# A recurrent attention with a mixing layer on one core: r and k of the first batch by token-parity halves, the logarithm of w and the last tile by halves, and a new order of the work

## The chip, the core and the metric

The kernel runs on one core of a Trainium2 chip. The core has five instruction queues that work side by side: TensorE (PE: matrix multiplies, and the loads of their weights), VectorE (DVE), ScalarE (ACT), GpSimd (POOL) and SyncE (SP, which here issues nearly all transfers). On-chip data lies in SBUF; PE writes its results into PSUM, from where DVE or ACT copies them ("evicts" them). The time is that of one execution on the device, in microseconds; a kernel is judged by the median of several runs.

## The reference

```python
state = zeros((B, H, D, D))                       # B 4, H 8, S 768, D 48
for t in range(S):                                # k, v, r: [B, H, S, D]; w, u: [H, D]
    cur = einsum('bhd,bhe->bhde', u[None] * k[:, :, t], v[:, :, t])
    y[:, :, t] = einsum('bhd,bhde->bhe', r[:, :, t], state + cur)
    state = w[None, :, :, None] * state + einsum('bhd,bhe->bhde', k[:, :, t], v[:, :, t])
x = y.transpose(0, 2, 1, 3).reshape(B, S, H * D)  # [4, 768, 384]
theta = x @ w_theta                               # [384, 384]
zr, zi = x * cos(theta), x * sin(theta)
yr = einsum('ts,bsd->btd', w_tok_r, zr)           # w_tok_r, w_tok_i: [768, 768]
yi = einsum('ts,bsd->btd', w_tok_i, zi)
u = x + yr + yi
out = u + maximum(u @ w_ch, 0)                    # [4, 768, 384], float32
```

## The kernel before

**Tiling.** The 768 tokens of a batch are three pairs of chunks of 128 tokens; with four batches there are twelve pairs, numbered g = 0 to 11. Within a pair the recurrence is turned into multiplies: r is scaled by powers of w (`wpow`) and k by inverse powers (`wpinv`, or `wpinvj` in the first batch), so that the decayed scores are a masked product of the two, and a 48x48 state per head is carried from chunk to chunk.

**One pair (`attention`).** r, k and v are loaded (`load_runs`, `load_kv`), r and k are scaled into `Rw` and `Kw` (L567, L580 and L583), PE transposes them in blocks of 128 by a multiply with the identity (`flips`, L530), and the results are evicted into `RT` and `KT` (L289 on ACT, L291 on DVE). Then come the scores (L631), their masks into `mAT` (L637), the elementwise product `PD` (L644, L650) and its head sums `dg` for the term with u (L659), `yd` (L666), the state updates (L690, evicted into `Sb`), the outputs (L730, L735) added into `x` (L742), the transposed `xT`, the product with w_theta (L760), its sine and cosine (L764, L767), and `zr`, `zi` (L770, L773). `xT` is made by PE for g under 6 and by a DMA transpose on SP after that (`turn`, L543).

**First batch.** In the first batch (`pj`) partition p of a loaded tile holds the tokens 2p and 2p+1 of a pair, side by side, for r, k and v. Index n is the parity of the token. The scales write both parities in one instruction of 128x768 elements; eight flips fill one PSUM tile of 128x1024 bf16, and one eviction writes them with the parities woven together. v is spread back to chunks by multiplies with a 0/1 matrix (`spread_v`, L615).

**Mixing (`mixing`).** The token weights are transposed by PE (L514). For each chunk, twelve multiplies (six parts of two, L791) sum both mixings in one PSUM tile; DVE adds x into `un` (L800); `un` is transposed into `uT`, by PE for g under 4 and for the last pair, by DMA otherwise; three multiplies with w_ch give f (L817); DVE takes the maximum with zero and adds `un` into `fin` (L821); SP stores it (L825). The last pair is flipped and stored one chunk at a time.

**Start.** w is loaded as one row and spread over the partitions by a float32 multiply with ones (L419), whose logarithm is taken in place in PSUM by ACT (L422). Six exponentials with a scale per partition (L428) make `wpow`, `wpinvj` and `wpinv`. `wS` (L454, POOL) scales the state.

**The order.** Each step is a task with its reads and writes. The table `ORDER` gives all tasks in the sequence in which they are issued, with the engine of each (0 PE, 1 DVE, 2 ACT, 3 POOL, 4 SP) and the PSUM tile of each result (eight tiles of 2 KB per partition). An engine runs its tasks in that sequence, each with its waits for its inputs and for the tile's previous reader. The costs and priorities in the task list have no effect on a table that is written out. Among PE's tasks stand 108 pairs of filler multiplies of zeros (`warm_up`, L834), most in the first 31 us and the rest near the end.

Of the kernel before, what the change touches and what calls it, by code (L numbers as in the profile page):

```python
# [15 lines left out]
F32 = mybir.dt.float32  # L16
BF16 = mybir.dt.bfloat16
Alu = mybir.AluOpType
# [9 lines left out]
    (0, 2), (4, 1), (13, 3), (2, 1), (3, 1), (16, 0, 7), (1, 2), (146, 4), (14, 3), (17, 0, 5),  # L28
    (7, 2), (145, 4), (8, 3), (10, 3), (9, 1), (32, 0, 2), (5, 1), (33, 0), (18, 2), (34, 0),
    (144, 4), (20, 2), (35, 0), (153, 3), (36, 0), (37, 0), (23, 2), (38, 0), (39, 0), (15, 3),  # L30
    (24, 2), (40, 0), (41, 0), (22, 2), (154, 0, 6, 0), (12, 3), (186, 4), (150, 1), (19, 2), (42,
    0), (21, 2), (11, 1), (43, 0), (6, 1), (44, 0), (25, 0, 3), (187, 4), (45, 0), (46, 0), (151,
    0, 5), (26, 1), (30, 1), (27, 2), (147, 1), (47, 0), (167, 0, 4), (152, 2), (48, 0), (49, 0),
    (50, 0), (168, 1), (51, 0), (188, 4), (52, 0), (53, 0), (28, 2), (54, 0), (155, 2), (55, 0),
    (189, 1), (31, 3), (56, 0), (148, 0, 3), (156, 2), (169, 0), (149, 2), (190, 0, 0), (229, 4),
    (192, 1), (57, 0), (58, 0), (59, 0), (191, 2), (60, 0), (61, 0), (157, 0, 1, 7), (170, 1),
    (62, 0), (63, 0), (163, 1), (64, 0), (228, 4), (193, 0, 6), (158, 1), (65, 0), (66, 0), (67,
    0), (195, 2), (68, 0), (69, 0), (164, 0, 5), (159, 1), (70, 0), (71, 0), (160, 0, 3, 4), (165,
    2), (194, 2), (230, 4), (166, 3), (196, 0, 1, 0), (161, 1), (72, 0), (73, 0), (209, 0, 7),
    (198, 2), (162, 1), (197, 2), (171, 0, 6), (140, 4), (234, 1), (74, 0), (210, 2), (75, 0),  # L40
    (76, 0), (202, 0, 3, 1), (29, 2), (199, 0, 0, 4), (172, 1), (231, 3), (173, 0, 5), (280, 4),
    (201, 1), (77, 0), (211, 0), (203, 1), (235, 0, 6), (272, 4), (237, 2), (78, 0), (79, 0),
    (174, 1), (80, 0), (81, 0), (82, 0), (83, 0), (212, 1), (84, 0), (236, 2), (232, 0, 4), (142,
    4), (205, 1), (85, 0), (86, 0), (87, 0), (251, 0, 7), (268, 4), (233, 2), (204, 1), (281, 3),
    (175, 0, 6), (200, 1), (88, 0), (141, 2), (206, 0, 1), (276, 4), (89, 0), (90, 0), (247, 1),
    (91, 0), (238, 0, 3, 0), (207, 2), (252, 2), (176, 1), (208, 3), (241, 0, 5, 4), (292, 4),
    (248, 0, 1), (240, 2), (243, 1), (213, 0, 7), (143, 2), (92, 0), (215, 0, 6), (242, 1), (249,
    2), (273, 2), (244, 0, 0, 4), (269, 3), (214, 1), (93, 0), (288, 4), (181, 0, 5), (239, 2),
    (216, 1), (270, 0, 1), (277, 2), (250, 3), (246, 1), (94, 0), (294, 4), (177, 0, 3), (271, 1),
    (182, 2), (217, 0, 4), (183, 2), (245, 1), (253, 0, 7), (293, 4), (218, 2), (297, 3), (95, 0),  # L50
    (96, 0), (97, 0), (254, 1), (278, 0, 6), (255, 0, 0), (178, 2), (184, 1), (282, 0, 4), (179,
    2), (284, 4), (256, 1), (223, 0, 5), (289, 2), (283, 1), (185, 3), (257, 0, 0), (296, 4),
    (180, 1), (219, 0, 7), (224, 2), (258, 2), (279, 1), (298, 0, 4), (98, 0), (274, 0, 3), (220,
    2), (333, 4), (300, 3), (99, 0), (221, 2), (100, 0), (290, 0, 0), (275, 1), (225, 2), (448, 0,
    6), (291, 1), (295, 4), (263, 0, 1), (299, 2), (222, 1), (449, 0), (285, 3), (441, 0, 0),
    (226, 1), (264, 2), (361, 4), (301, 0, 3), (265, 2), (227, 3), (259, 0, 4), (302, 1), (101,
    0), (442, 0), (260, 2), (266, 1), (443, 0), (363, 4), (261, 2), (450, 0), (310, 1), (267, 3),
    (286, 0, 1), (303, 2), (262, 1), (451, 0), (349, 4), (102, 0), (444, 0), (287, 1), (304, 0, 7,
    3), (307, 0, 4, 5), (314, 0, 1), (337, 4), (366, 3), (308, 1), (445, 0), (315, 2), (452, 0),
    (305, 1), (453, 0), (362, 4), (446, 0), (454, 1), (462, 0, 7), (311, 0, 4), (334, 3), (306,  # L60
    1), (463, 0), (357, 4), (312, 2), (350, 2), (464, 0), (447, 1), (313, 3), (465, 0), (466, 0),
    (402, 4), (316, 0), (335, 0, 4), (317, 1), (467, 0), (336, 2), (338, 3), (351, 0, 6), (468,
    1), (455, 0, 0), (352, 2), (318, 0, 3), (309, 1), (359, 4), (369, 3), (339, 0, 1), (367, 0,
    4), (319, 1), (345, 4), (340, 2), (320, 0, 7), (456, 1), (469, 0, 6), (368, 2), (321, 1),
    (470, 0), (341, 4), (370, 0, 0), (407, 3), (358, 2), (471, 0), (371, 1), (322, 0, 1), (364,
    4), (360, 2), (472, 0), (379, 1), (473, 0), (323, 2), (376, 0, 3, 7), (365, 4), (373, 0, 4,
    5), (346, 2), (377, 1), (474, 0), (324, 0, 0), (378, 1), (342, 2), (403, 4), (457, 0, 1),
    (475, 1), (328, 0, 7), (374, 1), (476, 0, 3), (404, 4), (329, 2), (380, 0, 6), (459, 0, 4),
    (477, 1), (381, 2), (325, 2), (375, 1), (343, 0, 6), (326, 2), (372, 3), (353, 4), (480, 0,
    3), (458, 1), (330, 2), (478, 0, 5), (327, 1), (382, 3), (344, 2), (347, 0, 1), (504, 4),  # L70
    (460, 1), (383, 0, 0), (348, 2), (479, 1), (408, 0, 6), (387, 0, 4), (481, 1), (384, 2), (410,
    3), (483, 0, 1), (331, 1), (405, 4), (484, 0), (409, 2), (388, 1), (389, 0, 5), (385, 0),
    (485, 0), (390, 1), (354, 2), (406, 4), (486, 0), (332, 3), (386, 1), (487, 0), (411, 0, 5),
    (505, 4), (355, 0, 3), (412, 1), (391, 0, 7), (509, 3), (356, 2), (488, 0), (420, 1), (506,
    4), (490, 0, 4), (392, 2), (414, 0, 6, 0), (417, 0, 5, 3), (415, 1), (491, 0), (544, 4), (413,
    3), (492, 0), (489, 1), (493, 0), (419, 1), (421, 0, 7), (494, 0), (495, 0), (422, 1), (416,
    1), (461, 4), (423, 3), (424, 0, 6), (510, 0, 1), (418, 1), (425, 2), (426, 0, 0), (507, 4),
    (496, 1), (511, 2), (629, 0, 3), (512, 3), (427, 1), (428, 0, 7), (622, 0, 5), (546, 4), (429,
    1), (103, 0), (397, 0, 0), (430, 0, 7), (398, 2), (497, 0, 1), (549, 3), (545, 4), (399, 2),
    (393, 0, 6), (431, 2), (513, 0, 4), (400, 1), (508, 4), (623, 0), (394, 2), (514, 1), (436, 0,  # L80
    7), (395, 2), (401, 3), (630, 0), (498, 1), (437, 2), (432, 0, 0), (547, 4), (396, 1), (438,
    2), (550, 0, 1), (522, 1), (433, 2), (499, 0, 6), (434, 2), (548, 4), (439, 1), (440, 3),
# [145 lines left out]
def pe_op(ns):  # L228
    return (ns, 217)
# [27 lines left out]
def build(ctx, tc, nc, r, k, v, w, u, moe_w_theta, moe_w_tok_r, moe_w_tok_i, moe_w_ch, out):  # L257
# [90 lines left out]
    def setup():  # L348
# [40 lines left out]
        def pads(ts):  # L389
            for t in ts:  # L390
                nc.gpsimd.memset(t[:, :, :, D:], 0.0)
# [494 lines left out]
```

## Time and profile before

| what | value |
|---|---|
| median of 5 runs | 140.5 us (139.0 to 140.79) |
| profiled execution | 138.66 us, of which span 137.0 us |
| granted TensorE clock, by the profile | 1.0 |
| PE, DVE, ACT, POOL busy in the span | 133.1, 106.9, 77.3, 86.3 us |
| the fillers, L834 | 216 multiplies |
| DMA | 27.6 MB, 202 GB/s mean |

The profile is of one execution. The page gives each engine's busy time, groups of instructions by line with their count, total and mean duration, and the idle time before them with what ended it. A multiply's duration contains its pipeline, so multiplies overlap and the distance between two starts is shorter than the duration of one: 163 ns for 384 columns and 56 ns for 128 columns at full rate. The chain goes back from the last instruction to what released it, and names what stood on the path at each time.

### The profile page before, as it was taken

The page shows a single profiled execution, that of the slowest core. Times are in us where ns is not written, and L with a number is a line of the kernel's source. Part 1 is how long each engine was busy: PE and PEld are TensorE (multiplying, and loading weights), DVE is VectorE, ACT ScalarE, POOL GpSimd, SP SyncE. Part 2 cuts the span into 40 slices and gives each one's busy share as a digit, 9 for nine tenths or more (in the row PEclk, how much of TensorE's full clock was granted, in tenths as well). Part 3 has the DMA queues.
Part 4 walks back from the last instruction along what each step waited for, and adds up shares of the span by engine and source line. Part 5 has one row for each costly group of instructions (what it writes and reads, how often), then busy time and mean ns, then how long its engine had stood idle before and what let it go on. Part 6 is the DMA issues. An engine that isn't in the chain of part 4 may idle for free.

```text
span 137.0 us, 4123 instructions
## 1 busy us (share of the span) xinstructions
PE 133.1 (97%) x1670; PEld 96.3 (70%) x1670; DVE 106.9 (78%) x208; ACT 77.3 (56%) x142; POOL 86.3 (63%) x77
## 2 busy tenths in 40 slices
PE   6999999999999999999999999999999997999995
PEld 4688798886678677686676866667677674666684
DVE  1399899988878898859986989797997897254750
ACT  3869799998559797379552429843018332310010
POOL 7703674999999199599999738689492084040000
PEclk9999999999999999999999999999999999999999
DMA  4999999999899999999999849598973947304761
GB/s 97 272 262 263 305 337 346 166 287 222 253 295 321 161 272 187 269 207 167 187 274 162 192 77 224 119 209 225 224 198 63 263 146 114 115 0 89 228 219 43
DMA packets 72445, 27.60 MB, mean 202 GB/s; under 512 B 67049, under 2 KB 70890, under 8 KB 72426
## 3 DMA queue, kind: packets, MB, share of 16 engines
q1 hardware_dynamic: 72400, 27.34, 87.3%
q8 instruction: 13, 0.21, 0.7%
q14 instruction: 6, 0.05, 0.1%
q10 hardware_dynamic: 26, 0.00, 0.0%
HBM read 20.06 MB, written 4.72 MB: 181 GB/s over the span
## 4 chain that ended last, share of the span: by engine, by line
PE 88%; DMA 8%; DVE 2%; ACT 0%; issue 0%; ACTq 0%; DVEq 0%
PE bank L791 30%; PE bank L530 11%; PE bank L834 10%; PE bank L760 8%; PE bank L817 8%; PE bank L631 4%; PE bank L690 4%; DMA uT<-un 3%; PE bank L735 3%; DMA xT<-x 3%; PE bank L514 3%; PE bank L730 2%; PE bank L659 2%; DVE mAT L637 1%; PE bank L419 1%; PE bank L615 1%
## 5 line engine op out<-in xcount | busy, mean ns | idle before, releaser
L791 PE MATMUL bank<-zi,WiT 128*128 128x384 bf16 x144 | 33.7, 326 | 0.0
L637 DVE TENSOR_TENSOR mAT<-bank,mask 128x512 bf16<-128x512 f32 x48 | 30.9, 681 | 3.5 <-PE bank L631 3.2
L791 PE MATMUL bank<-zr,WrT 128*128 128x384 bf16 x144 | 33.2, 326 | 0.0
L666 POOL TENSOR_TENSOR yd<-dg,vb 128x768 bf16<-128x768 f32 x12 | 18.1, 1506 | 18.0 <-ACT vb L289 6.2
L773 POOL TENSOR_TENSOR zi<-x,sin 128x768 bf16<-128x768 bf16 x12 | 19.7, 1641 | 6.2 <-ACT sin L764 5.9
L764 ACT ACTIVATE sin<-bank 128x384 bf16<-128x384 f32 x24 | 11.8, 496 | 14.9 <-PE bank L760 12.1
L567 POOL TENSOR_TENSOR Rw<-ld,wpow 128x768 bf16<-128x768 f32 x10 | 18.8, 1881 | 0.2 <-DVE mAT L637 0.2
L834 PE MATMUL bank<-zeros 128*128 128x128 bf16 x216 | 18.1, 231 | 0.0
L791 PEld LDWEIGHTS <-WiT 128*128 128x128 bf16 x144 | 12.8, 97 | 6.9
L791 PEld LDWEIGHTS <-WrT 128*128 128x128 bf16 x144 | 12.7, 97 | 6.9
L583 POOL TENSOR_TENSOR Kw<-ld,wpinv 128x768 bf16<-128x768 f32 x9 | 16.4, 1817 | 0.9 <-DMA ld<-in_k_dram 0.9
L770 DVE TENSOR_TENSOR zr<-bank,x 128x384 bf16<-128x384 f32 x24 | 13.0, 550 | 5.0 <-ACT bank L767 5.0
L821 DVE SCALAR_TENSOR_TENSOR fin<-bank,un 128x384 f32<-128x384 f32 x24 | 12.9, 551 | 4.4 <-PE bank L817 4.3
L834 PEld LDWEIGHTS <-zeros 128*128 128x128 bf16 x216 | 14.2, 103 | 3.0 <-issue 2.0
L817 PE MATMUL bank<-Wch,uT 128*128 128x384 bf16 x72 | 14.8, 326 | 0.8 <-DMA uT<-un 0.8
L760 PE MATMUL bank<-Wth,xT 128*128 128x384 bf16 x72 | 15.3, 326 | 0.1
L289 ACT ACTIVATE RT<-bank 128x1024 bf16<-128x1024 bf16 x12 | 12.3, 1031 | 5.3 <-PE bank L530 5.1
L800 DVE TENSOR_TENSOR un<-bank,x 128x384 bf16<-128x384 f32 x24 | 13.1, 551 | 2.2 <-PE bank L791 1.7
L742 DVE TENSOR_TENSOR x<-bank,yd 128x384 bf16<-128x384 f32 x24 | 12.8, 551 | 0.8 <-PE bank L735 0.6
L767 ACT ACTIVATE bank<-bank,pi 128x384 f32<-128x384 f32 x24 | 13.2, 565 | 0.0
L289 ACT ACTIVATE Sb<-bank 64x192 bf16<-64x192 f32 x20 | 6.5, 324 | 8.2 <-PE bank L690 8.0
L817 PEld LDWEIGHTS <-uT 128*128 128x128 bf16 x72 | 6.6, 98 | 4.8 <-DMA uT<-un 1.2
(96 smaller groups left out, 215.3 us busy)
## 6 DMA issues: line engine op xcount, KB each, us to landing
ld<-in_r_dram SPq DMA_DIRECT2D x12, 384.0 KB, 5.3
out_dram<-fin SPq DMA_DIRECT2D x11, 384.0 KB, 2.8
ld<-in_k_dram SPq DMA_DIRECT2D x18, 192.0 KB, 4.7
ld<-in_v_dram SPq DMA_DIRECT2D x18, 192.0 KB, 4.8
ld<-in_moe_w_tok_i_dram SPq DMA_DIRECT2D x6, 384.0 KB, 5.8
ld<-in_moe_w_tok_r_dram SPq DMA_DIRECT2D x6, 384.0 KB, 6.7
ld<-in_v_dram SPq DMA_DIRECT2D x3, 384.0 KB, 5.5
ld<-in_k_dram SPq DMA_DIRECT2D x3, 384.0 KB, 6.2
```

The costliest lines, as they stand in the source:

```text
L289: nc.scalar.activation(dst, src, Act.Copy)
L530: nc.tensor.matmul(bank16(tok)[:, i * C:(i + 1) * C], s, ident, is_transpose=True, start=(i == 0), stop=(i == n - 1))
L567: P.add(mul(g, 2.15), lambda e: eng_of[e].tensor_mul(Rw[:, :, :, :D].transpose([0, 2, 1, 3]), Ls[ir].rearrange("p (h n d) -> p h n d", h=H ...
L583: eng_of[e].tensor_mul(Kw[:, :, :, :D].rearrange("p a h d -> p (a h) d"), Ls[ik].rearrange("p (a d) -> p a d", d=D), wpinv.rearrange("p a ...
L637: P.add({DVE: dve_op(4 * C)}, lambda e, tk=tk[hi], c=c, hi=hi: nc.vector.tensor_mul(mAT[:, c, hi], bank(tk).rearrange("p (h t) -> p h t", ...
L666: P.add({POOL: pool_op(2 * HD, 1.7)}, lambda e: eng_of[e].tensor_mul(yd.rearrange("p a (h d) -> p (a h) d", h=H), wide(dg, D), vb.rearrang ...
L760: nc.tensor.matmul(bank(th)[:, :HD], xT[:, ND * c + dk, :], Wth[:, dk, :], start=(dk == 0), stop=(dk == ND - 1))
L767: P.add({ACT: act_op(HD, True, True)}, lambda e, th=th: nc.scalar.activation(bank(th)[:, :HD], bank(th)[:, :HD], Act.Sin, bias=pi2), use=[th],
L773: P.add({POOL: pool_op(2 * HD, 1.9)}, lambda e: eng_of[e].tensor_mul(zi[:, 2 * pr:2 * pr + 2], x[:, 2 * pr:2 * pr + 2], sn), rd=xk + [("si ...
L791: nc.tensor.matmul(bank(tm)[:, :HD], WT[:, so, to * C:(to + 1) * C], z[:, so], start=(so == 0 and part == 0), stop=(part == 2 * NP - 1 and ...
L817: nc.tensor.matmul(bank(tf)[:, :HD], uT[:, ND * t + dk, :], Wch[:, dk, :], start=(dk == 0), stop=(dk == ND - 1))
L834: nc.tensor.matmul(bank("warm")[:, :C], zeros, zeros, start=True, stop=True, skip_group_check=True)
```

## The change

**r and k of the first batch.** Each scale becomes two instructions, one per parity, of 384 elements each, which may run on DVE or POOL. Each half is flipped by four multiplies into a PSUM tile of its own, and evicted by itself, on ACT or DVE, into every second element of `RT` or `KT`. The keys of `Rw`, `Kw`, `RT` and `KT` are per parity. All later users wait for both halves. Pairs of the other batches are scaled and flipped as before.

**Logarithm of w.** The float32 multiply and the logarithm are done in two halves of 192 columns with a PSUM tile each; the logarithm goes into a new SBUF tile `lnw`, from which all six exponentials read.

**Last tile.** Chunk 1 of the last pair computes f in two column halves in two PSUM tiles, each with its own add and its own store.

**Order.** The whole table is new. The first loads are k, r, v of the first pair instead of v, k, r. Seven of the twelve scale halves stand on DVE and five on POOL (one of the second pair's k, all four of the third pair). 19 filler pairs stand before the first flip, 79 in all before the last multiply of f (before: 15 and 76), and 3 of them between the two halves of the last f. On SP the last stores are: second half of the last chunk, the chunk before it, first half of the last chunk. The planner's cost of a DMA transpose is changed from 1500 to 2000, which acts on nothing but the table.

```diff
+        for n in range(2):
+            q = slice(n * HD // 2, (n + 1) * HD // 2)
+            P.add({PE: pe_op(430)}, lambda e, n=n, q=q: nc.tensor.matmul(
+                bank(("w", n))[:, :HD // 2], ones, w_row[:, q], start=True, stop=True),
+                rd=["ones", "w_row"], wr=["wlog"], acq=[(("w", n), 1)], prio=-200)
+            P.add({ACT: act_op(HD // 2)}, lambda e, n=n, q=q: nc.scalar.activation(
+                lnw[:, q], bank(("w", n))[:, :HD // 2], Act.Ln),
+                rd=["table"], use=[("w", n)], wr=[("lw", n)], prio=-190)
...
-            P.add({ACT: act_op(HD, True, True)}, lambda e, i=i, dst=dst: nc.scalar.activation(
-                dst, bank("w")[:, :HD].rearrange("p (h d) -> p h d", h=H), Act.Exp,
+            P.add({ACT: act_op(HD, False, True)}, lambda e, i=i, dst=dst: nc.scalar.activation(
+                dst, lnw.rearrange("p (h d) -> p h d", h=H), Act.Exp,
                 scale=tok_f[:, i:i + 1]),
...
-        P.add({SP: (1600, 1500)}, lambda e: nc.sync.dma_start_transpose(out=dst, in_=src),
+        P.add({SP: (1600, 2000)}, lambda e: nc.sync.dma_start_transpose(out=dst, in_=src),
...
+    def mul1(g, rate):
+        return {POOL: pool_op(HD, rate), DVE: dve_op(HD)}
...
+        def halves(nm, w_key, wt, src4, ld, Xw, kx, XT, kxt, pri):
+            for n in range(2):
+                P.add(mul1(g, 2.15), lambda e, n=n: eng_of[e].tensor_mul(
+                    Xw[:, n, :, :D], src4[:, :, n, :], wt[:, :, n, :]),
+                    rd=L2(ld) + [(w_key, n)], wr=[kx[n]], prio=pri, lock=SHARED,
+                    name=nm[0].lower() + "scale")
+            for n in range(2):
+                flips(XT[:, :, :, n], [Xw[:, n, 2 * hp:2 * hp + 2, :] for hp in range(HP)],
+                      ("T" + nm[0], g, n), pri, [kx[n]], [kxt[n]], nm,
+                      {ACT: act_op(4 * C), DVE: dve_op(4 * C)})
...
         if pj:
             flat_kt = KT.rearrange("p a h t -> p (a h t)").rearrange("p (h m) -> p h m", h=HP)
-            flips(flat_kt.rearrange("p h (m n) -> p h m n", n=2),
-                  [Kw[:, n, 2 * hp:2 * hp + 2, :] for hp in range(HP) for n in range(2)],
-                  ("TK", g), pb, [kK], [kT], "KT", {ACT: act_op(8 * C)},
-                  lambda t: t.rearrange("q (h n) p -> q h p n", n=2))
+            halves("RT", "wpow", wpow, r4, ir, Rw, kRs, RTn, rt_keys, pb - 1)
+            halves("KT", "wpinvj", wpinvj, k4, ik, Kw, kKs,
+                   flat_kt.rearrange("p h (m n) -> p h m n", n=2), kTs, pb)
...
+                cut = 2 if g == B * NP - 1 and t == 1 else 1
+                for j in range(cut):
+                    tf = ("f", g, t, j)
+                    q = slice(j * HD // cut, (j + 1) * HD // cut)
+
+                    def chan(e, t=t, tf=tf, q=q):
+                        for dk in range(ND):
+                            nc.tensor.matmul(bank(tf)[:, :q.stop - q.start],
+                                             uT[:, ND * t + dk, :], Wch[:, dk, q],
+                                             start=(dk == 0), stop=(dk == ND - 1))
...
+                    if cut == 2:
+                        P.add({SP: (300, 2000)}, lambda e, t=t, q=q: nc.sync.dma_start(
+                            out=out[b, (2 * pr + t) * C:(2 * pr + t + 1) * C, q],
+                            in_=fin[:, t, q]), rd=[("fin", g % 2, t, j)],
+                            wr=[("out", g, t, j)], prio=-2e6, name="out")
```

## The prediction

> **What bounds the kernel now.** I read the page first (busy time, slices, groups), then the chain that ended last, then the timeline of the first 31 us and of the last 10.
>
> ```profile
> PE 133.1 (97%) x1670; PEld 96.3 (70%) x1670; DVE 106.9 (78%) x208; ACT 77.3 (56%) x142; POOL 86.3 (63%) x77
> PE 88%; DMA 8%; DVE 2%; ACT 0%; issue 0%; ACTq 0%; DVEq 0%
> L834 PE MATMUL bank<-zeros 128*128 128x128 bf16 x216 | 18.1, 231 | 0.0
> ```
>
> Busy share and chain both say PE. L834 is the filler: 108 pairs of multiplies of zeros, at fixed places in the order, so PE runs them whether or not it would have been idle. The chain, in order of time:
>
> ```profile
> 2.40 1.61 PE bank L419 x2
> 4.01 2.25 PE bank L834 x20
> ...
> 8.40 0.45 PE bank L530 x8
> ...
> 79.11 4.45 DMA xT<-x
> 83.61 0.66 PE bank L760 x3
> ...
> 111.68 4.51 DMA uT<-un
> 116.23 0.66 PE bank L817 x3
> ...
> 119.98 6.83 PE bank L791 x42
> ...
> 131.70 3.57 PE bank L834 x64
> ```
>
> To be seen: 64 fillers in 3.57 us are 56 ns each, the first 20 took 112 ns, and up to 8.2 us they stay slow, so PE starts at half rate. From there PE runs without a hole (42 mixing multiplies in 6.83 us, 163 ns each) but for two transposes by DMA. The end of the kernel is therefore a count of what stands in PE's order, plus its waits, plus what follows the last f.
>
> **The change, part by part.** The profiled execution took 138.66 us: its span of 137.0 and 1.66 around it. It lies 1.3% under the median of the runs (140.5), so I sum against 138.66 and carry the difference to 140.5.
>
> 1. *Logarithm by halves, r and k by halves.* The multiply L419 is two passes in 1.61 us; half of it ends near 3.2, so its logarithm (0.47 us whole, about 0.31 a half) is done while PE multiplies the other half, and the exponentials start near 4.4 instead of 4.56. Key loads now come first and should land at 4.4, when v landed before. The first scaled half of k can then be ready near 5.6 and both halves of r near 7.7 (384-element DVE operations take 0.55, half of a 0.95 scale 0.47 to 0.55); before they ended at 7.07 and 9.52. Does PE get there earlier? Before the first flip, PE's order now holds 19 filler pairs instead of 15 with the spreading of v and the small transpose between them. From 4.05, 38 multiplies at 0.107 (20 in 2.31, less the last one's length) end at 8.1: where the first flip stands today (8.24). The earlier data is thus worth nothing by itself; the fillers hide it, and they would hide a lateness of 0.9 us.
>
> 2. *PE's count to the last f.* At 8.2 us the kernel before has behind it 15 filler pairs, the spreading of v (0.33 at full rate) and the small transpose (0.20). The kernel after has 19 pairs and owes those 0.53. Ahead of its last f lie 79 pairs in all, not 76: 60 left against 61, less 0.11. Sum +0.42. Adding up the rows task by task to the first mixing multiply gives +0.15 instead, since some small gaps of today fall away. I take +0.3 (range 0 to 0.5). Halving flips adds no multiplies: eight of 56 ns become two times four; their evictions (1.02 us for 1024) become two of about 0.52 on ACT, or on DVE between 0.36 (half of the contiguous copy's 0.69) and 0.67 (the 512-element mask operation); I take the mask's, as the writes are strided.
>
> 3. *Scales on POOL.* Five of the twelve halves of r and k go to POOL: one of the second pair's k, then four of the third pair's in a row. A whole scale on POOL took 1.82, so a half is about 0.95. Two rows show more:
>
> ```profile
> 10.09 1.46 POOL L454 TENSOR_TENSOR wS<-wR,bmask 128x384 f32<-128x384 f32 x1 [3.77 <-ACT wR L441]
> 10.78 1.58 DVE L580 TENSOR_TENSOR Kw<-ld,wpinvj 128x768 bf16<-128x768 f32 x1
> 16.46 2.46 POOL L567 TENSOR_TENSOR Rw<-ld,wpow 128x768 bf16<-128x768 f32 x1 [0.22 <-DVE mAT L637]
> ```
>
> A 384-element multiply on POOL took 1.46 beside a DVE scale that itself took 1.58 instead of 0.95. The Trainium skill (SBUF — State Buffer, "Who interferes with whom") says that DVE with two SBUF inputs and POOL reading SBUF hold one port pair as a lock, the later waiting for the whole instruction, and that DVE with one SBUF input doesn't contend. The 2.46 fits: 1.82, plus the rest of a DVE scale that ran from 16.29 to 17.24. By the rule, the half of k at 10.6 (its load lands at 10.54, fifth as now) waits for DVE's scale of r, and PD (two SBUF inputs) then waits for it: PD ends near 12.5 instead of 11.6, the first mask near 13.1, and the flip that takes that mask's bank, at 12.7 in PE's order, waits 0.5. The four later halves lie beside masks, x and S, which read PSUM, and stay at 0.95. By the row of 1.46 alone the four would end at 15.6 + 5.84 = 21.4 and their flips wait 1.4 more. I take the rule, less what gaps give back: +0.3, bounds 0 and 2.0.
>
> 4. *New order in the middle.* The two DMA waits cost PE 0.81 (row of L817) and between 0.1 and 0.2 (at 83.6), up to 1.2 by the spacing of the multiplies; I take 1.0. PE work between the producing multiply and the first user, by durations of the rows: the xT of the eighth pair 5.3 us before, 6.9 after, so its wait goes. The uT of the ninth pair 4.6 before, with nearly 1.0 of wait, so 5.6 are needed; now 5.3: 0.3 stay. The last three (4.1, 4.2, 4.9 before, without a wait) are 4.4, 4.55, 4.55. A transpose took 2.7 to 4.5 us to land, so one of them can wait 0.5 where it doesn't today. SP's queue runs in order, and each transpose sits behind loads and stores that are ready before it in both orders. Everything else in the middle (evictions on DVE and ACT, bank reuse) is hidden by PE's work now and moves everywhere; I cost it at nothing, with 0.8 if a few come late. Sum -0.8, range -1.2 to +0.5.
>
> 5. *Tail.* Between the two half products of the last tile stand three filler pairs (in the count above), and DVE takes the second half's add first, then the whole tile, then the first half. From the last multiply, DVE ends after about 0.76 (the whole add of 0.55 is still running) against 0.66 today: +0.1. A half-size store follows:
>
> ```profile
> 131.25 1.11 DVE L821 SCALAR_TENSOR_TENSOR fin<-bank,un 128x384 f32<-128x384 f32 x2 [0.43 <-PE bank L817]
> 131.54 3.74 PE L834 MATMUL bank<-zeros 128*128 128x128 bf16 x64
> ```
>
> The last add ends at 132.36, the span at 137.0: 4.6 us are the store and the close. The skill (DMA: Bandwidth & Descriptors, "Anatomy of one DMA") fits a fixed 2.0 us plus bytes over 436 GB/s, for another queue's path; 98 KB less would save 0.22. The rows speak against it: 384 KB stores landed in a median 2.8 us, the two of 192 KB in 3.6. One more store in the row costs SP 0.34. I take -0.2, so -0.1 for the tail (range -0.4 to +0.4).
>
> Sum: +0.3 +0.3 -0.8 -0.1 = -0.3. 138.66 becomes 138.36; 140.5 becomes 140.2.
>
> **The rivals.**
> - *A, likeliest (0.51): gains and costs cancel.* 140.2, by itself 139.2 to 141.4. For it: PE's count is fixed, and fillers stand where the change would show.
> - *B, faster (0.27): the stalls go and nothing comes for them.* Port collisions fall beside fillers (0), waits -1.1, store by half its bytes -0.3, count +0.1: -1.3, so 139.2, down to 138.6. For it: all transposes but the last three have 5.3 us of work or more to cover them. Against: those three stay under 4.6.
> - *C, slower (0.22): the shared port in the first 22 us.* Four POOL halves in a row feed the third pair's flips; PE reaches the last r flip at 20.05. They start at 15.6, so it decides at a mean of 1.09 us each. At 1.46 they cost 1.4; the yd ahead of them may be late too (one took 1.84 instead of 1.48), say 0.2; with the earlier 0.5 that is 2.1 instead of 0.3: +1.5, so 142.0. Against: DVE does masks then.
> - *The halves do nothing at all* is inside A: step 1 already gives them no time.
>
> **How the numbers follow.** About 1% is what a measurement of this kernel can tell from no change (the five runs spread over 1.3%). B reaches under 139.1 about four times in five, C over 141.9 rather more than half the time, A seldom on either side. Faster 0.24, same 0.60, slower 0.16. The range takes A and most of B and C: 138.7 to 142.0.
>
> **What would show it.** Step 1: the first flip on PE stands within 0.3 of 8.2, with DVE's scales done before it. Step 2: the first mixing multiply at 30 to 31. Step 3: POOL halves near 0.95, one near 1.4, PD of the first pair ending after 12.2. Step 4: no wait of PE on xT of the eighth pair, under 0.5 on uT of the ninth. Step 5: the span ends 4.2 to 4.8 after the last add. The prediction is wrong if scores or flips of the second and third pair wait more than 1 us, if PE waits in the middle for evictions, or if the half-rate time of PE shifts by more than 1 us.

## The result, and the profile after

| | before | after |
|---|---|---|
| median of the runs beside each other | 139.62 us (79 runs, 137.85 to 141.08) | 138.87 us (44 runs, 137.86 to 139.62) |
| profiled execution, span | 138.66, 137.0 us | 139.27, 137.6 us |

After over before is 0.998, with a 95% interval from 0.9964 to 0.9995. A later set of runs gave 0.9933 (0.9911 to 0.9956), with medians of 139.02 and 139.79. All ratios leave out runs more than 1.5% above the fastest of their kernel: 30 of the 79 in the first set, by their times, and none in the later one. Over all runs of the first set the ratio of the means is 0.9945, and that of the medians 0.9946. So the change is a gain of between 0.05 and 0.9%, under the 1% bound of the forecast. It is real, and the forecast of no change missed it. The forecast difference was -0.3 us; the ratio of 0.998 makes it just that, and the medians differ by 0.75. The absolute 140.2 was too high from the start: the five runs that I had for the kernel before lay 0.9 above the median of 79. The fastest runs of the two kernels are equal (137.85 and 137.86) and the slowest are 1.46 apart, so in the main the change takes away long executions of the kernel before.

The two profiled executions point the other way: the one of the kernel before is among its faster ones, the one of the changed kernel is above its median. Much of what follows is about why they differ among themselves.

The page of the changed kernel: busy time, the chain's shares by engine, and the filler's group.

```profile
PE 134.0 (97%) x1675; PEld 98.7 (72%) x1675; DVE 109.6 (80%) x222; ACT 76.9 (56%) x140; POOL 85.5 (62%) x77
PE 81%; DMA 7%; DVE 6%; issue 2%; POOL 1%; ACT 1%; SPq 0%; DVEq 0%
L862 PE MATMUL bank<-zeros 128*128 128x128 bf16 x216 | 18.9, 238 | 0.0
```

PE is as busy as before, but DVE and POOL have 7% of the chain, not 2%. Its timeline from 5 to 14 us (start, duration, engine, line, operation; in brackets the idle time before it):

```profile
7.00 0.55 DVE L583 TENSOR_TENSOR Rw<-ld,wpow 128x384 bf16<-128x384 f32 x1
7.78 0.63 PE L535 MATMUL bank<-ident,Rw 128*128 128x128 bf16 x4
...
9.82 0.84 PE L862 MATMUL bank<-zeros 128*128 128x128 bf16 x12
...
10.58 1.00 POOL L583 TENSOR_TENSOR Kw<-ld,wpinvj 128x384 bf16<-128x384 f32 x1 [2.22 <-DMA ld<-in_k_dram]
10.62 1.84 DVE L583 TENSOR_TENSOR Rw<-ld,wpow 128x384 bf16<-128x384 f32 x2
12.39 0.68 DVE L659 TENSOR_TENSOR PD<-RT,KT 128x1024 bf16<-128x1024 bf16 x1
```

The first flip stands at 7.78, with both halves of r ready 0.23 before. PE runs at half rate until about 9.8 here (until 8.2 in the kernel before). Two DVE halves that should take 1.0 take 1.84 beside one POOL half, so PD ends at 13.07. The chain between 100 and 120 us:

```profile
102.57 5.23 DMA out_dram<-fin
...
112.38 4.67 DMA uT<-un
...
117.10 1.15 PE bank L835 x6
```

A store that took 5.23 us to land held DVE's next add for 1.52 us, and with it the masks and scores behind (PE stood 0.5 us near 108). The transpose for the ninth pair's f still took 4.67, but PE waited only 0.3 for it instead of 0.97. Last, the tail:

```profile
131.68 1.09 DVE L841 SCALAR_TENSOR_TENSOR fin<-bank,un 128x192 f32<-128x192 f32 x3 [0.61 <-PE bank L835]
...
132.06 3.40 PE L862 MATMUL bank<-zeros 128*128 128x128 bf16 x58
132.07 0.34 SPq L847 DMA_DIRECT2D out_dram<-fin  x1
132.53 1.55 SPq L853 DMA_DIRECT2D out_dram<-fin  x1
134.18 0.38 SPq L847 DMA_DIRECT2D out_dram<-fin  x1
```

SP needed 1.55 us, not 0.37, to issue the second of the three last stores, so the half store went out 1.4 us after its add (132.77), and the span ended 4.8 after that add.

### The profile page after: what moved, and what is told of

The parts are those of the page before. It is cut to its first block, busy times and chain, and to the rows that moved or that the text cites. A ratio compares the mean times of both kernels' runs of the same rounds, so it can differ in the third digit from the quotient of the medians.

```text
span 137.6 us, 4149 instructions
## 1 busy us (share of the span) xinstructions
PE 134.0 (97%) x1675; PEld 98.7 (72%) x1675; DVE 109.6 (80%) x222; ACT 76.9 (56%) x140; POOL 85.5 (62%) x77
## 4 chain that ended last, share of the span: by engine, by line
PE 81%; DMA 7%; DVE 6%; issue 2%; POOL 1%; ACT 1%; SPq 0%; DVEq 0%
PE bank L806 28%; PE bank L535 10%; PE bank L862 10%; PE bank L835 7%; PE bank L775 7%; PE bank L646 4%; DMA out_dram<-fin 4%; DMA uT<-un 3%; PE bank L750 3%; PE bank L519 3%; PE bank L705 3%; PE bank L745 2%; DVE mAT L652 1%; PE bank L674 1%; PE bank L424 1%
## 5 line engine op out<-in xcount | busy, mean ns | idle before, releaser
L862 PE MATMUL bank<-zeros 128*128 128x128 bf16 x216 | 18.9, 238 | 0.0
L841 DVE SCALAR_TENSOR_TENSOR fin<-bank,un 128x384 f32<-128x384 f32 (+1 forms) x25 | 13.0, 535 | 6.8 <-PE bank L835 5.2
L599 POOL TENSOR_TENSOR Rw<-ld,wpow 128x768 bf16<-128x768 f32 x9 | 16.3, 1817 | 3.3 <-DMA ld<-in_r_dram 3.3
L291 ACT ACTIVATE RT<-bank 128x1024 bf16<-128x1024 bf16 (+1 forms) x14 | 12.7, 924 | 6.3 <-PE bank L535 6.1
L862 PEld LDWEIGHTS <-zeros 128*128 128x128 bf16 x216 | 14.9, 108 | 1.6 <-issue 0.7
L835 PE MATMUL bank<-Wch,uT 128*128 128x384 bf16 (+1 forms) x75 | 15.3, 320 | 0.1
L782 ACT ACTIVATE bank<-bank,pi 128x384 f32<-128x384 f32 x24 | 13.2, 559 | 0.0
L775 PEld LDWEIGHTS <-xT 128*128 128x128 bf16 x72 | 6.5, 97 | 3.6
```

The source lines that it names most:

```text
L599: P.add(mul(g, 2.15), lambda e: eng_of[e].tensor_mul(Rw[:, :, :, :D].transpose([0, 2, 1, 3]), r4, wpow), rd=L2(ir) + [("wpow", 0), ("wpow" ...
L775: nc.tensor.matmul(bank(th)[:, :HD], xT[:, ND * c + dk, :], Wth[:, dk, :], start=(dk == 0), stop=(dk == ND - 1))
L782: P.add({ACT: act_op(HD, True, True)}, lambda e, th=th: nc.scalar.activation(bank(th)[:, :HD], bank(th)[:, :HD], Act.Sin, bias=pi2), use=[th],
L835: nc.tensor.matmul(bank(tf)[:, :q.stop - q.start], uT[:, ND * t + dk, :], Wch[:, dk, q], start=(dk == 0), stop=(dk == ND - 1))
L841: nc.vector.scalar_tensor_tensor(fin[:, t, q], bank(tf)[:, :q.stop - q.start], 0.0, un[:, t, q], op0=Alu.max, op1=Alu.add),
L862: nc.tensor.matmul(bank("warm")[:, :C], zeros, zeros, start=True, stop=True, skip_group_check=True)
```

## The experiments

Ratios are to the kernel before, with 95% intervals. In the trace, a queue of its own carries packets of 16 KB, one for about every 256 instructions of PE (198 to 311 by count in the kernel before) and 13 in all for PE's 1675 multiplies and as many weight loads: PE's program. The Trainium skill (Runtime: NRT & Kernel Launch, "Instruction fetch mechanics") states such a refill in 16 KiB blocks of 256 instructions, by DMA; the count here agrees. "Theory F" is that these fetches hold up transfers.

**The tail, and the kernel without any filler.** The second and third kernel were meant to lose only the fillers behind the last f:

```diff
-                for _ in range(2):
+                for _ in range(0 if i >= 76 else 2):     # kernel before; 79 in the changed kernel
```

The function runs after its loop has ended, when `i` is 107, so both kernels lost all 108 pairs. The expectations speak of the smaller edit. The first kernel has no edit; the fourth stores the last tile whole:

```diff
-                        P.add({SP: (300, 2000)}, lambda e, t=t, q=q: nc.sync.dma_start(
-                            out=out[b, (2 * pr + t) * C:(2 * pr + t + 1) * C, q],
-                            in_=fin[:, t, q]), ...
+                        P.add({SP: (300, 2000)}, lambda e, t=t, j=j: j or nc.sync.dma_start(
+                            out=out[b, (2 * pr + t) * C:(2 * pr + t + 1) * C, :],
+                            in_=fin[:, t]), ...
```

> The changed kernel unaltered, as the yardstick for its variants on the same chip. Every theory: 0.998 of the kernel before, 0.995 to 1.001. What differs between executions is shown by its profile: theory F (fetch in the tail, see the next kernel) expects again a 16-KB packet of the instruction queue near the start of the last stores and a span that ends over 4.6 us after the last add; rival N (the tail of the first profile was a chance) expects the two half stores of the last tile to be issued 0.35 us apart and the span to end 4.2 to 4.5 after the last add.

> The kernel before without the 32 filler pairs that stand behind its last f (64 multiplies of zeros, 3.6 us of PE; nothing is computed in them). Theory F: PE's program is fetched in 16-KB packets, one for about every 256 of its instructions, and the last of them runs 0.96 us on one DMA engine at 132.79, between the packets of the last store; without the fillers PE never comes to it, the last store lands about 0.8 earlier, and the time falls by 0.5 to 1.0 us (0.993 to 0.996). Rival P: the fillers themselves end last (135.3, with 1.7 us of close), so the time falls by more, down to the landing of the store: 1 to 2 us (0.986 to 0.993). Rival N: the end is the store and it is as long as before: within 0.2 us (0.999 to 1.001).

> The changed kernel without the 29 filler pairs behind its last f. Theory F: the 16-KB packet that ran 1.52 us at 132.20 goes or comes elsewhere, the second store of the last tile is issued 0.35 after the first instead of 2.1, and the time falls by 1.0 us, between 0.6 and 1.4 (0.990 to 0.996 of the changed kernel). As PE's instruction count ends right at the point where that packet was asked for, it may still be fetched; then it is seen in the trace and nothing is gained. Rival P: as for the kernel before, 1 to 2 us. Rival N: within 0.2 us.

> The changed kernel with the last tile stored whole, by one store after both half adds, instead of by two half stores. My prediction's step (half the bytes in the last store are worth 0.2 us): 0.2 us slower than the changed kernel. Theory F: what the half store gains is lost in SP's issue, which stood behind the first half's; so 0.0, between 0.4 faster and 0.2 slower. Rival H (half stores are worth more, two stores of half a tile overlap fully): 0.4 to 0.6 slower.

Measured: the changed kernel again 139.02 (0.9933). Without any filler the kernel before took 135.74 (0.972, 0.9677 to 0.9762) and the changed one 136.13 (0.9727, 0.9692 to 0.9762). One whole store: 138.91 (0.9928, 0.9906 to 0.995), no difference. What follows: the half stores are worth nothing that these runs can tell, and the 108 pairs that I had counted into both sums cost 2.8% in the kernel before and about 2.1% in the changed one; without them six runs of each show no gain from the change (135.65 to 137.07 and 135.59 to 136.19). From the page and the timeline of the changed kernel without fillers:

```profile
q8 instruction: 11, 0.18, 0.6%
```

```profile
7.24 0.59 PE L535 MATMUL bank<-ident,Rw 128*128 128x128 bf16 x4 [3.41 <-DVE ident L389]
...
130.65 0.34 SPq L847 DMA_DIRECT2D out_dram<-fin  x1
131.12 0.38 SPq L853 DMA_DIRECT2D out_dram<-fin  x1
131.60 0.39 SPq L847 DMA_DIRECT2D out_dram<-fin  x1
```

Eleven packets instead of thirteen, stores issued 0.47 apart, and a first flip only 0.5 earlier than behind 19 filler pairs. The first mixing multiply stands at 30.71 here, and at 30.55 and 31.38 in the two profiles with fillers. Yet PE stayed at half rate for much longer: until about 18 us here (four flips took 0.60 at 15.43 and 0.40 at 18.37), and until about 21 in the kernel before without fillers, where eight flips, 0.61 at full rate, took:

```profile
19.33 1.04 PE L530 MATMUL bank<-ident,Kw 128*128 128x128 bf16 x8
```

So 13 us for this, in an expectation further down, is too early.

**The fillers behind the last f alone, the scales whole, a third result buffer.**

```diff
-            def warm(e):
-                for _ in range(2):
+            def warm(e, i=i):
+                for _ in range(0 if i >= 76 else 2):     # kernel before; 79 in the changed kernel
```

```diff
-    (30, 2), (166, 1), (203, 3), (65, 0), ...
+    (30, 2), (166, 1), (203, 1), (65, 0), ...             # second pair's k on DVE
...
+                first = n == (1 if g == 0 else 0)
-                P.add(mul1(g, 2.15), lambda e, n=n: eng_of[e].tensor_mul(
-                    Xw[:, n, :, :D], src4[:, :, n, :], wt[:, :, n, :]),
+                P.add(mul1(g, 2.15), lambda e, first=first: first and eng_of[e].tensor_mul(
+                    Xw[:, :, :, :D].transpose([0, 2, 1, 3]), src4, wt),
```

```diff
-    fins = ring(2, [C, 2, HD], F32, "fin")
+    fins = ring(3, [C, 2, HD], F32, "fin")                # and g % 3 wherever fin is used
```

> The kernel before, with the 32 filler pairs behind its last f left out and the other 76 kept. In the two kernels without any filler the last store was written 1.6 to 1.7 us after the last add instead of 2.9 to 3.3, PE's program was fetched in 11 packets of 16 KB instead of 13, and the time fell by 3 to 4 us. Theory F (the fetch of the fillers' own code lies between the packets of the last store): this kernel has 12 packets, none of them in the tail, its last store lands 1.6 to 1.9 us after the last add, and the time falls by 1.2 to 1.7 us (0.988 to 0.992). Rival M (fillers slow the store by being run, not by being fetched): the same time, but with a 16-KB packet after 130 us. Rival Q (what was gained without fillers was PE's count alone): within 0.3 us (0.998 to 1.002).

> The changed kernel, with the 29 filler pairs behind its last f left out and the other 79 kept. Theory F: as for the kernel before, 1.2 to 1.7 us less than the changed kernel (about 0.983 to 0.987 of the kernel before); the last two stores are issued 0.5 apart. Rival Q: within 0.3 us of the changed kernel (0.993 to 0.997 of the kernel before). If the change's tail is worth what my step 5 says (-0.1 us), the two kernels without trailing fillers differ by the head and the middle alone: 0.5 to 0.7 us.

> The changed kernel with one part undone: the logarithm starts when both halves of the multiply are done, and the scales of r and k of the first batch are done whole by one instruction each, at the place of the first half (the second pair's k on DVE, so that POOL takes no part in it). Flips and their evictions stay halves, and the order stays. Step 1 of my prediction (fillers hide the earlier data) expects 0.0, between 0.2 faster and 0.2 slower than the changed kernel (0.993 to 0.997 of the kernel before), with the first flip within 0.4 us of where it was. Rival D: the head is set by the data and not by PE's count, since without any filler PE reaches the first mixing multiply at 30.7 to 31.2, where it also is with 79 pairs; then the halves are what brought the first mixing multiply forward by 0.4, and this kernel is 0.3 to 0.6 us slower than the changed one (0.997 to 1.000 of the kernel before).

> The changed kernel with three buffers for the result of f instead of two, so that an add into one no longer waits for the store of two steps earlier. In the profile of the changed kernel such a wait held DVE 1.52 us at 106.4, and PE stood still about 0.7 us for the masks behind it. Theory W (this new wait is what ate the middle's gain): the wait is gone and the time falls by 0.5 to 0.8 us (0.989 to 0.992 of the kernel before). Rival Y: the wait moves on to the transpose by DMA behind it, or is seldom as long as in that profile: 0 to 0.2 us (0.993 to 0.995).

Measured: without the trailing fillers 138.18 us (0.9856, 0.9792 to 0.9921) for the kernel before and 137.26 (0.9812, 0.9763 to 0.9862) for the changed one, with 12 packets each, the last at 116.2 and 114.2. The last data landed 1.6 us after the last add, as theory F says; between the two medians 0.9 us remain, more than the 0.5 to 0.7 expected, but from six runs each, whose intervals overlap.

Whole scales: 139.58 (0.998, 0.9956 to 1.0004), nearer to rival D: 0.2 us slower than the changed kernel by the medians, 0.6 by the ratios given here. (The edit left the logarithm as it was: ACT still began its first half at 3.24.) The first flip did not move (7.78), so as to the first data step 1 was right. PE lost its time later: it waited 0.65 at 13.0 for DVE, where a whole scale now stood ahead of a small product. This edit also took POOL's half of the second pair's k to DVE, and the same move alone cost the changed kernel 1 us in the last experiment; so what the halves are worth by themselves stays open.

Third buffer: 138.38 (0.9909, 0.9872 to 0.9947). DVE's wait for the store is gone from its profile, but from the first mixing multiply to the last it took 97.34 us, against 97.36 in the second profile of the changed kernel: the wait went to the transpose (0.45 at 116), as the rival says. The median is better than this explains, and its interval reaches the changed kernel's; that stays unclear.

**Shifting the fetches.** In the ten profiles so far, transposes for f after 75 us landed after a median 2.8 us (39 of them) without a fetch in between and 4.6 (11) with one. Leaving out ten pairs ahead of the first flip moves every later fetch by 40 instructions. The third kernel keeps PE busy in the tail with fewer, wider multiplies.

```diff
-            def warm(e):
-                for _ in range(2):
+            def warm(e, i=i):
+                for _ in range(0 if i < 10 else 2):       # "or i >= 79" in the last two
...
+                if 79 <= i < 99:                          # wide tail alone
+                    nc.tensor.matmul(bank("warm")[:, :HD], zeros, Wch[:, 0, :], start=True, stop=True,
+                                     skip_group_check=True)
```

> The changed kernel without the first 10 of the 19 filler pairs ahead of the first flip: 40 instructions of PE fewer, all at a time when PE waits for data anyway. In every trace with all fillers, a 16-KB packet of PE's program ran at 103.0 to 104.6 (for 0.9 to 1.7 us), while a store of f landed 5.1 to 5.4 us after its issue, and another at 113.9 to 115.9, while a transpose by DMA landed after 4.4 to 4.8; stores and transposes that met no such packet landed after a median 2.7 and 2.8. Theory F: with 40 instructions fewer the two packets come 3 to 3.5 us later (near 106.3 and 117.4), miss that store and that transpose, which then land after about 2.8; PE's waits at 108 and 116 (0.5 to 0.8 together) go, and the time falls by 0.5 to 0.8 us (0.989 to 0.992 of the kernel before). The packet in the tail comes about 1.1 us later, still among the last stores. Rival S (the landing is slow because of what else moves at that place): the waits stay, and the time is within 0.2 us of the changed kernel. Rival G (the fillers ahead of the first flip warm PE's clock): the granted clock comes later, the first mixing multiply is 0.5 or more late, and the time rises.

> The kernel before without the first 10 of its 15 filler pairs ahead of v's spreading. Theory F: the packet that ran at 114.15, while the transpose for the ninth pair's f landed after 4.51 us and PE waited 0.97 for it, comes near 117.4; the transpose lands after 2.8, the wait goes, and the time falls by 0.8 to 1.2 us (0.991 to 0.994). Rival S: within 0.2 us (0.999 to 1.001). Rival G: slower.

> As the changed kernel with 10 filler pairs fewer at the head, and with the 58 filler multiplies of 128 columns behind the last f replaced by 20 of 384 columns: PE runs fillers for the same 3.3 us, with 76 instructions fewer, so that its program should end before the next 16-KB packet is asked for. Theory F: no packet after 120, the last two stores are issued 0.5 apart and land 1.6 to 1.9 after the last add, and the time is 1.2 to 1.7 us under the kernel with 10 pairs fewer alone. Rival M (multiplies that run slow the store or the end): as slow as that kernel, within 0.3, although no packet is fetched; or, if it is PE's own end that closes the kernel, in between.

> As the changed kernel with 10 filler pairs fewer at the head, and without the 29 pairs behind its last f. Both theories: 1.2 to 1.7 us under the kernel with 10 pairs fewer alone. Theory F: no difference to the kernel with wide fillers in the tail beyond 0.3 us. Theory F for the whole sum: the waits at 108 and 116 gone (0.5 to 0.8) and the tail's (1.7): 136.3 to 136.8 us, about what the changed kernel took without any filler (136.13).

Measured: 138.89 (0.9915, 0.9892 to 0.9939); 139.38 for the kernel before (0.9988, 0.9958 to 1.0018); wide tail 137.38 (0.9828, 0.9775 to 0.988); no tail 137.47 (0.9823, 0.977 to 0.9877). The changed kernel with ten pairs fewer, in its chain between 100 and 119 us:

```profile
105.98 0.49 PE bank L835 x3
107.69 0.49 PE bank L835 x3
114.34 0.97 PE bank L835 x6
117.27 0.97 PE bank L835 x6
```

No transfer is left in it. The fetches ran at 106.8 and 116.9, the transpose landed after 2.98 us instead of 4.4 to 4.8, and PE had no wait above 0.15 us in the middle; the kernel before likewise lost its wait of 0.97. In the traces theory F holds against rival S. The sum did not follow, since rival G is right too: PE ran at half rate until 12.7, the remaining fillers in the head took twice their time, and the first mixing multiply came at 32.11 instead of 30.55 to 31.38. Gain and loss cancel. The wide tail's end:

```profile
132.05 3.41 PE L865 MATMUL bank<-Wch,zeros 128*128 128x384 bf16 x20
132.05 0.34 SPq L847 DMA_DIRECT2D out_dram<-fin  x1
132.52 0.37 SPq L853 DMA_DIRECT2D out_dram<-fin  x1
132.99 0.40 SPq L847 DMA_DIRECT2D out_dram<-fin  x1
```

PE runs fillers for the same 3.4 us, but with 12 packets, and the last data landed 1.63 us after the last add, as without fillers, against 3.2 in the kernel with ten pairs fewer alone. So it is the fetch of the fillers that holds the last stores, not their running.

**The kernel before again, and only the first fillers.** The first two have no edit. The others keep 19 pairs of the changed kernel and 15 of the kernel before.

```diff
-            def warm(e):
-                for _ in range(2):
+            def warm(e, i=i):
+                for _ in range(2 if i < 19 else 0):       # 15 in the kernel before
```

> The kernel before unaltered, for its profile. Theory C (the head pays for a late clock): if PE runs at full rate from T us, its first mixing multiply starts near 30.6 + (T - 7.8), so 31.0 at 8.2 and 32.6 at 9.8, while the changed kernel has 30.55 + 0.35 (T - 7.8). Rival K (the kernel before is late for another reason, for instance its loads): the first mixing multiply does not go with T; at T over 9.5 it is still under 31.6.

> The same as the run before it, for one more point of T and of the first mixing multiply: theory C 30.6 + (T - 7.8), rival K under 31.6 at any T.

> The changed kernel with only its first 19 filler pairs, those ahead of the first flip, and without the other 89. Theory C: PE is at full rate from 7.8 to 10 us instead of 13, without the fillers that it then runs at half rate between the data; the first mixing multiply is no later than 30.7 and the time is 0 to 0.5 us under that of the changed kernel without any filler: 135.6 to 136.1, unless a fetch meets a transpose that PE waits for (then up to 136.9). Rival D (the data alone set the head): 136.1 within 0.2, with the first mixing multiply at 30.7.

> The kernel before with only its first 15 filler pairs, those ahead of v's spreading. Theory C: 0 to 0.6 us under that of the kernel before without any filler: 135.1 to 135.7, with the first mixing multiply at 30.6 to 31.2. Rival D: 135.7 within 0.2. If here too the changed order is 0.2 to 0.5 slower, then without the fillers' fetches the change is a small loss, and its gain in the full kernel is owed to them.

Measured: in the two executions (139.89 and 140.02) full rate began at about 7.6 and 6.9, and the first mixing multiply stood at 31.00 and 31.82. Theory C says 30.4 and 29.7 for these; for this kernel it falls. (In the changed kernel the two do go together: 30.55, 30.56, 30.79, 31.22 and 31.38 with full rate from 7.9, 7.8, 8.5, 9.4 and 9.8, in the five profiles with all the head's fillers and its scales as they were.) With only the first fillers: 138.24 (0.9881, 0.9817 to 0.9944) and 137.75 (0.9843, 0.9792 to 0.9894), two us more than with none. The granted clock shows one possible reason, which no run isolates. It fell again when the fillers stopped, between 17 and 27 us (a tenth of full speed per step, 40 slices):

```profile
PEclk9999985699999999999999999999999999999999
```

That is the kernel before with 15 pairs; the changed one has 6, 5, 8 in its fifth to seventh slice. The second execution of the unaltered kernel before shows another cause. From its timelines between 14 and 20.5 us:

```profile
14.68 1.47 POOL L666 TENSOR_TENSOR yd<-dg,vb 128x768 bf16<-128x768 f32 x1 [4.38 <-ACT dg L289]
...
16.11 1.81 POOL L567 TENSOR_TENSOR Rw<-ld,wpow 128x768 bf16<-128x768 f32 x1
16.20 2.54 DVE L580 TENSOR_TENSOR Kw<-ld,wpinvj 128x768 bf16<-128x768 f32 x1
18.67 0.54 DVE L742 TENSOR_TENSOR x<-bank,yd 128x384 bf16<-128x384 f32 x1
```

```profile
19.26 0.61 PE L530 MATMUL bank<-ident,Kw 128*128 128x128 bf16 x8 [0.81 <-DVE x L742]
```

The prediction shows the same POOL scale in the profile of before, at 16.46, with 2.46 us. There DVE had begun first:

```profile
16.29 0.95 DVE L580 TENSOR_TENSOR Kw<-ld,wpinvj 128x768 bf16<-128x768 f32 x1
```

In the second execution POOL began 0.09 us ahead, POOL took 1.81, DVE 2.54, and PE waited 0.81. Of the five profiles of this order with most of its fillers, POOL was first in three and DVE in two, the one I predicted from among these. The meeting is not all of the spread: DVE was first in the other execution, which took 139.89 all the same. It had its first mixing multiply 0.8 earlier, and lost that to waits for transposes and in the tail.

**The two meetings.**

```diff
+            if g == 2:
+                nc.gpsimd.memset(idle, 0.0)               # 128x256 bf16, ahead of the third pair's r scale
```

```diff
-    (30, 2), (166, 1), (203, 3), (65, 0), ...
+    (30, 2), (166, 1), (203, 1), (65, 0), ...             # second pair's first k half on DVE, alone
```

> The kernel before with one memset of 256 bf16 columns (0.28 us, of a tile that nothing reads) on POOL ahead of the third pair's scale of r, so that POOL comes to that scale about 0.2 us after DVE has begun the second pair's scale of k. Theory L (the meeting of the two scales costs the kernel before 0.9 us whenever POOL is first, which it was in three of five profiles with fillers): DVE's scale stays at 0.95, POOL's takes 2.3 to 2.6, PE does not wait for x near 18.4, and the median falls by 0.4 to 0.6 us, the upper end of the runs from 141 to 140.2 (0.995 to 0.998). Rival K (the spread of the runs comes from the loads or from PE's clock): within 0.2 us, with the same spread.

> The changed kernel with the first half of the second pair's k scaled on DVE instead of POOL, at the same place of the order. Step 3 of my prediction (that half meets DVE's two-input work at 10.7 us and costs 0.3 us): DVE's r halves take 1.0 together and PD 0.68, PD ends near 11.6 to 12.0 instead of 12.2 to 13.1, and the time falls by 0.2 to 0.4 us against the changed kernel (0.990 to 0.993 of the kernel before, where the changed one stood at 0.9945 by the medians). Rival: the half on DVE costs as much as the meeting, or the wait is hidden: within 0.1 us.

Measured: the kernel before with POOL a little later took 139.14 (0.9932, 0.9906 to 0.9958), so one memset brings it where the changed kernel stands. Its timeline:

```profile
17.04 0.31 POOL L570 MEMSET idle<- 128x256 bf16 x1
17.14 0.95 DVE L584 TENSOR_TENSOR Kw<-ld,wpinvj 128x768 bf16<-128x768 f32 x1
17.31 2.46 POOL L571 TENSOR_TENSOR Rw<-ld,wpow 128x768 bf16<-128x768 f32 x1
18.00 0.55 DVE L746 TENSOR_TENSOR x<-bank,yd 128x384 bf16<-128x384 f32 x1
```

The fall of the median is what theory L says, at about twice its size. This one profile shows DVE first, as meant, but not the gain: PE came to full rate only at 9.3, and the first mixing multiply stood at 31.66. So the gain rests on the medians. The changed kernel with its k half on DVE took 140.36 (1.0003, 0.9972 to 1.0034), 1 us slower than the changed kernel, where both expectations saw no loss. PD ended at 11.95 as expected, but everything behind it on POOL came sooner too:

```profile
14.39 1.48 POOL L681 TENSOR_TENSOR yd<-dg,vb 128x768 bf16<-128x768 f32 x1 [1.40 <-ACT dg L291]
14.46 1.82 DVE L583 TENSOR_TENSOR Kw<-ld,wpinvj 128x384 bf16<-128x384 f32 x1
```

```profile
16.93 0.36 PE L750 MATMUL bank<-vb,mAT 128*128 128x48 bf16 x8 [1.20 <-DVE mAT L652]
```

POOL's `yd` now began 0.07 ahead of DVE's other k half (0.24 behind it in the changed kernel's profile), and the half took 1.82 instead of 0.56. The same happened in the changed kernel with only 19 pairs (1.79 us, PE waiting 1.93), which is the other reason for its time.

## Why the prediction was wrong

- **From the sum to "the same" (wrong).** I took 1% as what a measurement can tell from no change, after five runs. With 79 and 44 runs the interval is 0.3% wide, and a gain of 0.2% shows. By the ratio of 0.998 the sum of -0.3 was right, by the medians it was 0.45 too small; that it came so near is luck, as the terms below show.
- **What bounds the kernel (wrong).** I read the end as a count of what stands in PE's order. Without any filler PE reached the first mixing multiply at 31.18 (before) and 30.71 (changed), where it also was with 138 and 148 filler multiplies ahead of it, although it then ran at half rate until 18 us or later. The head is set by DVE, POOL and ACT as much as by PE; a filler there costs nothing when PE is at full rate and something when it is at half rate.
- **Step 1 (right in the main).** Both halves of r were ready before the first flip, which was set by the fillers. It stood at 7.78, 0.4 from the 8.2 that I named, not within 0.3. That the halves' being early is worth nothing is not settled: the run with whole scales changed another thing too.
- **Step 2 (+0.3, wrong in kind).** The first mixing multiply was to stand at 30 to 31; it stood at 31.38, and at 30.55 in the second profile. But 14 transposing multiplies (8 flips, 6 of the token weights), 0.78 us, had been moved behind it, so the head was later than it seems, and the count was not what set it.
- **Step 3 (+0.3, the step that failed).** The rule was right. PD ended after 12.2 (13.07; 12.24 in the second profile), the four late POOL halves took 0.97 each, PE waited 0.3. What failed is the base. I took the 2.46 of POOL in the profile of before as a harmless row. It was one of two outcomes of a meeting decided by less than 0.2 us, and three of five profiles have the other one. The Trainium skill (SBUF — State Buffer, "Who interferes with whom") says that issue order, not the operation's shape, decides who blocks; the pairs 0.95 and 2.46, 2.54 and 1.81 agree. The changed order has no such meeting at that place; it has a smaller one at 10.6, where POOL's half was ahead of a DVE half in the profile after and behind both in the second. In place of +0.3 this step should have read between +0.3 (DVE first) and -0.5 (POOL first, 0.8 later at the first mixing multiply). The price of the meeting was measured in the kernel before (0.9932 with the memset alone). That the gain of the change is this term is inferred from its size and not shown: it was not isolated in the changed kernel, and step 4's gain is as large.
- **Step 4 (-0.8, right).** PE's waits for transposes between the first mixing multiply and the last were 1.20, 1.65 and 1.45 us in the three profiles of the unaltered kernel before, and 0.30 and 0 in the two of the changed one. From the first to the last it took 97.8 us before, and 97.6 and 97.4 after, with those 14 multiplies more and 6 fillers fewer (+0.44): 0.6 to 0.9 less waiting. The transpose for the ninth pair's f was no faster (4.67 us after, 4.51 before), so it was PE's longer work in between that covered more of it, as I had said. What I did not know is why it takes that long, a fetch of PE's program, and a store held up by another fetch brought a wait that I had put at nothing (0.5 of PE near 108 in the first profile).
- **Step 5 (-0.1, nothing).** The span ended 4.8 after the last add, then 4.5 in the second profile, 4.6 before. One whole store did as well. The term that matters there is the fetch of the trailing fillers, 1.4 to 1.9 us in the medians. Both kernels have it, and the prediction does not.
- **Rivals.** C named the shared port, but in the changed kernel, and on the slow side. The cases of its kind did arise, with one operation moved or the fillers gone (PE waiting 1.2 and 1.9). A, the cancelling, was right in sign and small; its terms were not those that cancelled.

No version was run that joins the two gains found here, the kernel before with no filler and with the memset. Without fillers that kernel still had the meeting in its profile (DVE 2.57), so whether the gains add up is open. The fastest of all runs were the kernels without fillers.

## What to carry over

Where two instructions on DVE and POOL that both read SBUF become ready within some tenths of a microsecond, a profile shows one of two kernels; ask for the other outcome's price before you call a long row harmless, and separate them on purpose. Fillers are code: before they are added (or counted), look where their fetches fall, and what the kernel does without them. And take the profile of a second execution of the unaltered kernel before a sum is made against the first.

## What the runs showed of the hardware

- A 16-KB packet of PE's program took 0.9 to 1.8 us on one DMA engine. In ten profiles transposes for f that met one landed after a median 4.6 us instead of 2.8, and stores after 4.4 instead of 2.7. SP's own issue of one of the last stores took 1.3 to 1.8 us instead of 0.4 in the four profiles in which a packet had begun just before it.
- Two instructions on DVE and POOL that read SBUF (DVE's with both inputs there) held each other up for all but 0.1 us of the whole instruction: 0.95 became 2.54 behind a POOL scale of 1.81, and 1.82 became 2.46 behind DVE.
- PE's change to full rate came between 6.9 and about 10 us with all fillers in the head, at 10.6 to 13.2 with ten pairs fewer, and at about 18 and 21 with none; the Trainium skill (TensorE: Matmul & The Clock Gate, Part 1) has it follow a window that runs freely, which fits the spread. The page's row of granted clock does not show it: where a page has the row, it starts with 9. It fell to 5 only in the two kernels with the first fillers alone.
